# wq and w1 in one load each, 128 rows of w2 on four DMA engines, and softmax sums carried in the o product

## The chip, the cores and the metric

The kernel runs on one core of a Trainium2 chip. The metric is the device time of one execution in microseconds (us), the median of several runs. The engines are TensorE (PE), VectorE (DVE), ScalarE (ACT), GpSimd (POOL) and SyncE (SP). SP issues nearly all transfers here; 16 DMA engines carry them out.

## What is computed

The reference is one decode step of a layer whose attention and MLP stand side by side: x + A(xn) + B(xn), with xn the layernorm of x. x has 2 rows (B = 2) of D = 576.

```python
xn = (x - mean(x)) / sqrt(var(x) + 1e-5)
# A: attention over the last W = 2048 positions of the caches; 32 query heads share 16 kv heads
q = xn @ wq                                # [576, 4096]
p = softmax(q @ k.T * 128 ** -0.5)         # k, v: 2 x 16 heads x 2048 x 128
A = (p @ v) @ wo                           # [4096, 576]
# B: MLP with a squared relu
h = relu(xn @ w1 + b1) ** 2                # [576, 4608]
B = h @ w2 + b2                            # [4608, 576]
```

All inputs and the output are bf16.

## The kernel before, in words

**Units.** Attention is cut into 8 units (`NU`), each of 4 kv heads of one of the two rows; a unit's k and v are one DMA of 2 MB each into one of 6 buffers of `kvpool`. For unit u, `step(u)` (line 473) transposes k on PE as pairs of bf16 seen as f32 (32 matmuls into `kT_ps`, 3 PSUM buffers, line 289), copied out by ACT and DVE in turn (lines 297 and 299), multiplies it with the queries (`scores`), and forms the softmax (`softmax`, line 316): a maximum per partition on DVE (`mx`), a maximum over partitions on POOL (`gmax`), `nb` on DVE, exp on ACT (`pr`, with its row sums), and a 32x32 transpose on DVE (`pT`).

**The product with v** lags two units behind. `pv_sum(u)` (line 337) adds the softmax sums over partitions with an f32 matmul with `samec`, takes the reciprocal (`ri`) and makes the factors `f`. `pv(u, i)` multiplies into `pv_ps`, one PSUM buffer. `pv_mix(u)` (line 359) brings four parts together on DVE, each with its column of `f`: instructions `acc` at lines 365 and 368. `pv_out(u)` (line 377) puts the result in head order into `sm` by an f32 matmul with `tohead`; after every fourth unit `od` and `ws` are formed from it on DVE, and `wo_acc` (line 393) multiplies with one half of wo into `out_ps`. `sm` is one PSUM buffer, shared by units 0 to 3 and then by units 4 to 7.

**The weights wq and w1** (576 rows) are loaded by `issue_w` (line 114) in three DMAs: 512 rows at 4 rows to a partition in two DMAs of two rows each, and the last 64 rows as two half rows (`wq_rem`, `w1_rem`, named `w_rem` in the trace). `q_block(c)` (line 254) and `mlp_h_block(c)` (line 407) multiply each of the five pieces as it comes.

**The MLP.** `mlp_h_end` (line 415) takes relu on ACT and the square on DVE into `hrow` (bf16), transposes it in 9 PE instructions (`ha`), and copies it to `hT_sb`. w2 is in 4 groups of 9 rows to a partition. The first three go into `out_ps` (`mlp_o`), which is copied to `part` (line 541). The last group comes in two DMAs (7 and 2 rows to a partition) and goes into `tail_ps` (`mlp_tail`), where `part` is added by matmuls with the identity. Two engines copy `tail_ps` out and store it (lines 548 to 553).

**Order.** PE's instructions keep the order of the program text (`pe_mm` and `pe_tr`, lines 89 to 93, which is why most matmuls have the line 90 or 93), and so do the instructions of `pv_mix`. The other engines' order is made by the tile scheduler. SP issues in the order k0, wq, k1, v0, k2, v1, k3, then one v and one k for each step as buffers come free, wo's first half, w1, the last k, v and v, wo's second half, and w2. After `step(6)` stand `mlp_h_start`, the products of units 4 and 5, `wo_acc(0)`, h, `step(7)`, the products of units 6 and 7, `wo_acc(1)`, and w2 (lines 524 to 546).

Of the kernel before, what the change touches and what calls it, by code (L numbers as in the profile page):

```python
# [11 lines left out]
ALU = mybir.AluOpType  # L12
# [4 lines left out]
def kernel(  # L17
# [39 lines left out]
    NFULL = D // P  # L57
    RW = 2
    REM = D - NFULL * P
    S = P // REM  # L60
    KC = NFULL + 1
    NXN = NFULL + S
    LQ = (Hq * Dh) // S
    L1 = F // S
    NG4 = 4
    QW = Hq * Dh // NG4
    QB = QW // 2
    QH = QW // Dh
# [3 lines left out]
    RB = 32 * (NG4 - 1) + B  # L72
# [9 lines left out]
    wbig = ctx.enter_context(tc.tile_pool(name="wbig", bufs=NFULL // RW))  # L82
    wrem = ctx.enter_context(tc.tile_pool(name="wrem", bufs=1))
# [14 lines left out]
    k_tiles, v_tiles, wq_tiles, w1_tiles, wo_tiles, w2_tiles = {}, {}, {}, {}, {}, {}  # L98
    WBW = max(Hq * Dh, F)
    WRW = max(LQ, L1)  # L100
# [13 lines left out]
    def issue_w(tiles, wt, i, name, width, lrem):  # L114
        if i < NFULL // RW:
            tl = wbig.tile([P, RW * WBW], BF16, tag="wbig", name=f"{name}_{i}")
            rows = wt[0:NFULL * P, :].rearrange("(p r) n -> p (r n)", r=NFULL)
            nc.sync.dma_start(out=tl[:, 0:RW * width], in_=rows[:, i * RW * width:(i + 1) * RW * width])
            for r in range(RW):
                tiles[i * RW + r] = tl[:, r * width:(r + 1) * width]  # L120
        else:
            tl = wrem.tile([P, WRW], BF16, tag="wrem", name=f"{name}_rem")
            nc.sync.dma_start(out=tl[:, 0:lrem], in_=wt[NFULL * P:D, :].rearrange("r (s l) -> (r s) l", s=S))
            tiles[NFULL] = tl

    def issue_wq(c):
        issue_w(wq_tiles, A_wq, c, "wq", Hq * Dh, LQ)

    def issue_w1(c):
        issue_w(w1_tiles, B_w1, c, "w1", F, L1)  # L130

    def w_rows(tiles, c, col0, n, L):
        if c < NFULL:
            return tiles[c][:, col0:col0 + n], c
        sg = col0 // L
        assert (col0 + n - 1) // L == sg
        return tiles[c][:, col0 - sg * L:col0 - sg * L + n], NFULL + sg
# [9 lines left out]
    def issue_w2(g, r0, r1):  # L147
        if g < NG4 - 1:
            tl = kvpool.tile([P, FR * D], BF16, tag="kv", name=f"w2_{g}")[:]
        else:  # L150
            if r0 == 0:
                w2_last.append(wbig.tile([P, FR * D], BF16, tag="wbig", name=f"w2_{g}"))
            tl = w2_last[0][:, r0 * D:r1 * D]
        rows = B_w2[g * HW:(g + 1) * HW, :].rearrange("(p r) n -> p (r n)", r=FR)
        nc.sync.dma_start(out=tl, in_=rows[:, r0 * D:r1 * D])
        w2_tiles[(g, r0)] = tl

    x_sb = const.tile([B, D], BF16, name="x_sb")
    nc.scalar.dma_start(out=x_sb[:], in_=x2d)
# [6 lines left out]
    NW = NFULL // RW + 1  # L166
    for i in range(NW):
        issue_wq(i)
    ones_f = const.tile([P, P], F32, name="ones_f")
    nc.vector.memset(ones_f[:], 1.0)  # L170
    col_f = const.tile([P, P], F32, name="col_f")
# [12 lines left out]
    ones_b = const.tile([1, B], BF16, name="ones_b")  # L184
    nc.vector.memset(ones_b[:], 1.0)
# [3 lines left out]
    for i in range(2):  # L189
        nc.vector.bn_stats(out=stats[:, i, :], in_=x_sb[:, i * half_d:(i + 1) * half_d])  # L190
# [6 lines left out]
    xn_sb = const.tile([B, D], BF16, name="xn_sb")  # L197
    nc.vector.tensor_scalar(out=xn_sb[:], in0=x_sb[:], scalar1=mv[:, 0:1], scalar2=rstd[:, 0:1],  # L198
                            op0=ALU.subtract, op1=ALU.mult)
    xr_sb = const.tile([B, S, P], BF16, name="xr_sb")  # L200
    nc.vector.memset(xr_sb[:], 0.0)
    for sg in range(S):
        nc.vector.tensor_copy(out=xr_sb[:, sg, sg::S], in_=xn_sb[:, NFULL * P:D])

    pro_ps = psum.tile([P, NXN, B], BF16, tag="misc", name="pro_ps")
    for c in range(NFULL):
        pe_tr(out=pro_ps[:, c, :], in_=xn_sb[:, c:NFULL * P:NFULL], identity=ident[:B, :B])
    for sg in range(S):
        pe_tr(out=pro_ps[:, NFULL + sg, :], in_=xr_sb[:, sg, :], identity=ident[:B, :B])
    xnT = const.tile([P, NXN, B], BF16, name="xnT")  # L210
    nc.vector.tensor_copy(out=xnT[:], in_=pro_ps[:])
# [21 lines left out]
    samec = const.tile([P, P // NC, NC], F32, name="samec")  # L233
    nc.gpsimd.tensor_copy(out=samec[:], in_=own[:].unsqueeze(1).to_broadcast([P, P // NC, NC]))
    tohead = const.tile([P, NC, DW], F32, name="tohead")
    nc.gpsimd.tensor_copy(out=tohead[:], in_=own[:].unsqueeze(2).to_broadcast([P, NC, DW]))
    qz = const.tile([P, 2, NU, 2, 4, NC], BF16, name="qz")
# [16 lines left out]
    def q_block(c):  # L254
        for k in range(2):
            for g in range(NG4):
                rhs, xc = w_rows(wq_tiles, c, g * QW + k * QB, QB, LQ)
                pe_mm(q_ps[k][32 * g:32 * g + B, :], lhsT=xnT[:, xc, :], rhs=rhs,
                                 start=(c == 0), stop=(c == KC - 1), skip_group_check=True,
                                 tile_position=(0, 32 * g))  # L260
        if c == KC - 1:
            qrow = const.tile([RB, QW], BF16, tag="row", name="qrow")
            nc.vector.tensor_copy(out=qrow[:, 0:QB], in_=q_ps[0][0:RB, :])
            nc.scalar.copy(out=qrow[:, QB:QW], in_=q_ps[1][0:RB, :])
            qT_ps = psum.tile([P, QH, P], BF16, tag="misc", name="qT_ps")
            for i in range(QH):
                pe_tr(out=qT_ps[:, i, 0:RB], in_=qrow[:, i * Dh:(i + 1) * Dh],
                                    identity=ident[0:RB, 0:RB])
            qT_v = qT_ps[:].rearrange("p i (g s) -> p i g s", s=32)
            for b in range(B):  # L270
                nc.vector.tensor_copy(out=qT_all[:, b, :].rearrange("p (g i) -> p i g", g=NG4), in_=qT_v[:, :, :, b])
            qe_ps = psum.tile([P, 2 * NU, NC], F32, tag="sm", name="qe_ps")
            for e in range(2):
                pe_mm(qe_ps[:, e * NU:(e + 1) * NU, :], lhsT=par[:, e, :, :].rearrange("p a i -> p (a i)"),
                                 rhs=qT_all[:].rearrange("p b h -> p (b h)"), start=True, stop=True)
            for a, cp in ((0, nc.vector.tensor_copy), (1, nc.scalar.copy)):
                lo, hi = a * (P // 2), (a + 1) * (P // 2)
                for w in range(2):
                    cp(out=qz[lo:hi, :, :, w, 2 * w + a, :].rearrange("p e u c -> p (e u) c"), in_=qe_ps[lo:hi, :, :])

    kT_tiles, sc_tiles, pT_tiles, sum_tiles, sm_tiles = {}, {}, {}, {}, {}
# [34 lines left out]
    def softmax(u):  # L316
# [12 lines left out]
        sums = keep.tile([P, 1], F32, tag="sums", name=f"sums_{u}")  # L329
        nc.scalar.activation(out=pr[:], in_=sc_ps, func=ACT.Exp, bias=nb[:], scale=scale, accum_out=sums[:])  # L330
        pT = keep.tile([P, NT, 32], BF16, tag="pT", name=f"pT_{u}")
        nc.vector.transpose(out=pT[:].rearrange("p t m -> p (t m)"), in_=pr[:])  # L332
        pT_tiles[u], sum_tiles[u] = pT, sums
# [3 lines left out]
    def pv_sum(u):  # L337
        tq, b = divmod(u, B)
        if u % (2 * B) == 0:
            sm_tiles[tq // 2] = psum.tile([P, B * Dh + 2 * B], F32, tag="sm", name=f"sm_{tq // 2}")  # L340
        rs = sm_tiles[tq // 2][:, B * Dh + u % (2 * B):B * Dh + u % (2 * B) + 1]
        pe_mm(rs, lhsT=samec[:].rearrange("p x c -> p (x c)"), rhs=sum_tiles.pop(u)[:],
                         start=True, stop=True, skip_group_check=True)
        f = work.tile([P, 4], F32, tag="f", name=f"f_{u}")
        ri = work.tile([P, 1], F32, tag="ri", name=f"ri_{u}")
        nc.vector.reciprocal(out=ri[:], in_=rs)
        nc.vector.tensor_scalar(out=f[:], in0=own_j[:], scalar1=ri[:, 0:1], scalar2=None, op0=ALU.mult)
        pv_cur[u] = (psum.tile([P, 4, Dh], F32, tag="misc", name=f"pv_ps_{u}"), f)

    def pv(u, i):  # L350
        pv_ps, f = pv_cur[u]
        v = v_tiles[u][:].rearrange("p (w t x) -> p t w x", w=2, t=NT)
        for k in range(4):
            t = 4 * i + k
            pe_mm(pv_ps[32 * k:32 * (k + 1), :, :].rearrange("m (w a) d -> m w (a d)", w=2),
                                  lhsT=pT_tiles[u][:, t, :], rhs=v[:, t, :, :], start=(i == 0),
                                  stop=(i == NT // 4 - 1), skip_group_check=True, tile_position=(0, 32 * k))

    def pv_mix(u):
        pv_ps, f = pv_cur[u]  # L360
        acc = None
        for j in range(4):
            nx = work.tile([P, Dh], F32, tag=f"acc{j % 2}", name=f"acc_{u}_{j}")
# [220 lines left out]
```

## Time and profile before

| what | value |
|---|---|
| median of 9 runs (lowest, highest) | 134.63 us (134.44, 135.23) |
| the profiled execution: time, span | 134.62 us, 132.8 us |
| PE busy | 92.9 us, 70% of the span |
| DVE, ACT, POOL busy | 61.6, 46.4, 7.4 us |
| moved by the DMA engines | 53.74 MB, mean 405 GB/s |
| mean granted clock of PE | 0.871 |

The profile is of one execution on the chip; its span is from the first to the last instruction that it shows. Busy time is not the same as what sets the end: for that the chain of waits is followed back from the last instruction, and the rows in order of time tell when each instruction started, how long it took, and what ended the idle time before it. A matmul's row has a start and a duration; several in a row are merged, with their count behind "x". "PEld" is a load of the stationary operand, which overlaps PE. The granted clock is the share of full speed at which PE was allowed to run in a stretch.

### The profile page before, as it was taken

Reading aid. Unit: us, or ns where it says so; the run is one execution under the profiler, and the core shown is the slowest. Engines: PE = TensorE matmul, PEld = TensorE weight load, DVE = VectorE, ACT = ScalarE, POOL = GpSimd, SP = SyncE. Lnnn points to the kernel's source line nnn. Section 1 sums busy time; section 2 is a strip of 40 time slices with the busy share of each in tenths; the row PEclk is TensorE's granted clock in tenths of the full one; section 3 lists DMA queues with packets and bytes.
Section 4 is the critical chain, followed back from the end, with each engine's and each line's share of the span. In section 5 each row is a group of like instructions: output and inputs, shape, how many; then the busy total and the mean of one; then the engine's idle time right before and its main releaser. Section 6 shows DMA issues by size and latency. Waiting matters only on the chain.

```text
span 132.8 us, 2075 instructions
## 1 busy us (share of the span) xinstructions
PE 92.9 (70%) x846; PEld 56.4 (42%) x846; DVE 61.6 (46%) x169; ACT 46.4 (35%) x63; POOL 7.4 (6%) x20
## 2 busy tenths in 40 slices
PE   0059744986499779779689619977967973829761
PEld 0059412753464535445345305434526931305530
DVE  6914404455424665664763761367322448260021
ACT  6705503394353355364373253332032542000001
POOL 7500000100100010010000100001000001000000
PEclk9999999599658999999999975698698699555999
DMA  4999999999999999999999999999999999999940
GB/s 149 386 432 429 429 434 419 434 424 434 427 434 429 434 429 424 434 429 434 419 424 439 427 443 427 427 433 427 418 439 419 439 428 433 417 428 425 420 203 1
DMA packets 4260, 53.74 MB, mean 405 GB/s; under 512 B 530, under 2 KB 536, under 8 KB 1052
## 3 DMA queue, kind: packets, MB, share of 16 engines
q1 hardware_dynamic: 4180, 53.61, 95.0%
q8 instruction: 6, 0.10, 0.3%
q0 software_dynamic: 64, 0.01, 0.0%
q14 instruction: 2, 0.02, 0.0%
q10 hardware_dynamic: 8, 0.00, 0.0%
HBM read 53.62 MB, written 0.00 MB: 404 GB/s over the span
## 4 chain that ended last, share of the span: by engine, by line
DMA 46%; PE 32%; DVE 9%; issue 3%; ACT 3%; SPq 2%; POOL 1%; ACTq 0%; POOLq 0%
DMA w<-in_B_w_dram 23%; DMA k<-in_A_k_cache_dram 23%; PE kT_ps L93 15%; PE sc_ps L90 6%; PE pv_ps L90 5%; DVE kT L299 3%; DVE mx L319 3%; PE out_ps L90 2%; ACT kT L297 2%; PE h_ps L90 2%; SPq L111 1%; DVE acc L368 1%; PE sm L90 1%; POOL gmax L323 1%; PE tail_ps L90 1%
## 5 line engine op out<-in xcount | busy, mean ns | idle before, releaser
L93 PE MATMUL kT_ps<-ident_f,k 128*128 128x128 f32 x256 | 44.6, 326 | 5.5 <-DMA k<-in_A_k_cache_dram 3.8
L297 ACT COPY kT<-kT_ps 128x1024 bf16<-128x1024 bf16 x32 | 31.9, 1012 | 31.5 <-PE kT_ps L93 31.5
L93 PEld LDWEIGHTS kT_ps<-ident_f,k 128*128 128x128 f32 x256 | 34.9, 167 | 18.1 <-issue 8.1
L299 DVE COPY kT<-kT_ps 128x1024 bf16<-128x1024 bf16 x32 | 22.0, 687 | 31.2 <-PE kT_ps L93 31.2
L90 PE MATMUL sc_ps<-kT,qz 128*32 128x512 bf16 x128 | 9.8, 388 | 6.4 <-DVE kT L299 5.5
L90 PE MATMUL pv_ps<-v,pT 128*32 128x512 bf16 x128 | 13.7, 472 | 0.0
L330 ACT ACTIVATE pr<-sc_ps,nb 128x512 bf16<-128x512 f32 x8 | 5.5, 687 | 20.4 <-DVE nb L327 20.3
L90 PE MATMUL sm<-acc,tohead 128*64 128x128 f32 x16 | 3.9, 333 | 6.9 <-DVE acc L368 6.9
L323 POOL PARTITION_ALL_REDUCE gmax<-m x8 | 2.9, 366 | 101.8 <-DVE m L321 82.0
L368 DVE SCALAR_TENSOR_TENSOR acc<-pv_ps,f,acc 128x128 f32<-128x128 f32 x24 | 8.3, 346 | 0.5
L332 DVE STREAM_TRANSPOSE pT<-pr 128x512 bf16<-128x512 bf16 x8 | 5.7, 709 | 4.8 <-ACT pr L330 4.8
L90 PE MATMUL out_ps<-wo,ws 128*2 128x288 bf16 x64 | 7.1, 407 | 1.1 <-DVE ws L390 1.1
L319 DVE TENSOR_REDUCE mx<-sc_ps 128x1 f32<-128x512 f32 x8 | 5.5, 692 | 3.5 <-PE sc_ps L90 3.1
L552 ACT CAST fin_sb<-tail_ps 2x144 bf16<-2x144 f32 x2 | 0.5, 273 | 17.8 <-PE tail_ps L90 17.8
L90 PEld LDWEIGHTS <-qz 128*32 128x32 bf16 x128 | 2.1, 94 | 10.1 <-DVE kT L299 7.1
L90 PEld LDWEIGHTS <-ws 128*2 128x2 bf16 x64 | 3.8, 118 | 4.7 <-DVE ws L390 1.5
L90 PEld LDWEIGHTS sm<-acc,tohead 128*64 128x64 f32 x16 | 1.7, 152 | 9.6 <-DVE acc L368 8.8
L90 PE MATMUL sm<-sums,samec 128*128 128x1 f32 x16 | 3.5, 289 | 2.8 <-DVE od L386 2.8
L90 PEld LDWEIGHTS <-pT 128*32 128x32 bf16 x128 | 3.2, 99 | 4.4 <-issue 3.9
L93 PE MATMUL pro_ps<-ident,xn_sb 2*128 2x2 bf16 x4 | 0.3, 172 | 6.7 <-DVE xn_sb L198 6.7
L90 PEld LDWEIGHTS sm<-sums,samec 128*128 128x128 f32 x16 | 3.0, 238 | 4.5 <-DVE od L386 3.0
L541 DVE COPY part<-out_ps 2x288 f32<-2x288 f32 x2 | 0.9, 448 | 7.9 <-PE out_ps L90 7.9
(86 smaller groups left out, 63.2 us busy)
## 6 DMA issues: line engine op xcount, KB each, us to landing
k<-in_A_k_cache_dram SPq DMA_DIRECT2D x8, 2048.0 KB, 22.2
v<-in_A_v_cache_dram SPq DMA_DIRECT2D x8, 2048.0 KB, 26.0
wo<-in_A_wo_dram SPq DMA_DIRECT2D x2, 2304.0 KB, 22.6
w<-in_B_w_dram SPq DMA_DIRECT2D x2, 2304.0 KB, 29.9
wq<-in_A_wq_dram SPq DMA_DIRECT2D x2, 2048.0 KB, 14.0
w<-in_B_w_dram SPq DMA_DIRECT2D x3, 1296.0 KB, 26.3
w<-in_B_w_dram SPq DMA_DIRECT2D x1, 1008.0 KB, 30.9
w_rem<-in_B_w_dram SPq DMA_DIRECT2D x1, 576.0 KB, 33.3
```

What stands on the lines that cost most here:

```text
L90: return tc.keep_in_program_order(nc.tensor.matmul(out, **kw))
L93: return tc.keep_in_program_order(nc.tensor.transpose(**kw))
L111: return [lambda i=i: nc.sync.dma_start(out=tl[:, i * n:(i + 1) * n], in_=v[:, :, i * n:(i + 1) * n]) for i in range(parts)]
L297: nc.scalar.copy(out=dst, in_=src)
L299: nc.vector.tensor_copy(out=dst, in_=src)
L319: nc.vector.tensor_reduce(out=mx[:], in_=sc_ps, axis=AX.X, op=ALU.max)
L323: nc.gpsimd.partition_all_reduce(gmax[:], m2[:], channels=P, reduce_op=ReduceOp.max)
L330: nc.scalar.activation(out=pr[:], in_=sc_ps, func=ACT.Exp, bias=nb[:], scale=scale, accum_out=sums[:])
L332: nc.vector.transpose(out=pT[:].rearrange("p t m -> p (t m)"), in_=pr[:])
L368: op = nc.vector.scalar_tensor_tensor(out=nx[:], in0=pv_ps[:, j, :], scalar=f[:, j:j + 1], in1=acc[:], op0=ALU.mult, op1=ALU.add)
L541: nc.vector.tensor_copy(out=part[:, i * OH:(i + 1) * OH], in_=out_ps[32 * i:32 * i + B, :])
L552: cp(out=fin_sb[:, q * OQ:(q + 1) * OQ], in_=mlp["out"][32 * k:32 * k + B, :])
```

## The change

wq and w1 become one DMA each. A weight matrix of 576 rows is seen as 1152 half rows, 9 to each of the 128 partitions, in one contiguous run; an odd and an even half row can belong to the same row of the matrix, so `xnT` holds 9 columns for each of two halves, with zeros where a partition's half row belongs to the other. The products of the two halves come out in different rows of PSUM (4 rows where there were 2). For q they are added within a matmul in f32 with a selection matrix (`sel_q`); for h, `hrow` is f32 and is transposed in f32, and `add_halves` adds the halves behind it; relu and square follow in one DVE instruction.

The last 128 rows of w2 leave the last group (now 8 rows to a partition, in DMAs of 6 and 2). They go into `w2x_sb`, 48 partitions of which 32 are used, by two DMAs that ACT issues early, with an outermost dimension of 4 on the side of the source. Their part of h is copied apart (`hx`), and eight matmuls (`mlp_x`) add their product to `out_ps` ahead of the other groups.

The softmax sums are stored as a 129th column beside the mixed product (`acc`), and the matmul with `tohead` carries them; the reciprocal is taken once in four units, and `od` is formed by two instructions. `pv_sum`, `samec`, `f` are gone; `pv_mix` takes the factors `own_j`. Biases and x are added in one product with `res_b`, and b1 and b2 are loaded through ACT's queue.

```diff
-    def issue_w(tiles, wt, i, name, width, lrem):
...
+    def issue_w(wt, name, width):
+        tl = wbig.tile([P, HP * FL], BF16, tag="wbig", name=f"{name}_sb")
+        nc.sync.dma_start(out=tl[:, 0:HP * width], in_=wt.rearrange("d (s l) -> (d s) l", s=2)
+                          .rearrange("(p r) l -> p (r l)", r=HP))
+        w_tiles[name] = tl
...
+    def q_all():
+        w = w_tiles["wq"]
+        for k in range(HP):
             for g in range(NG4):
+                o = k * QL + g * QB
+                pe_mm(q_ps[k % 2][32 * g:32 * g + 2 * B, :], lhsT=xnT[:, k, :, :].rearrange("p a b -> p (a b)"),
+                      rhs=w[:, o:o + QB], start=(k < 2), stop=(k >= HP - 2), skip_group_check=True,
+                      tile_position=(0, 32 * g))
+        qrow = const.tile([RB, 2, QB], F32, tag="row", name="qrow")
...
+        for i in range(QH):
+            for k in range(2):
+                pe_mm(qs_ps[:, i, :], lhsT=qrow[:, k, i * Dh:(i + 1) * Dh],
+                      rhs=sel_q[0:RB, k, :, :, :].rearrange("p b h g -> p (b h g)"), start=(k == 0), stop=(k == 1))
...
-    def pv_sum(u):
...
+    def pv_start(u):
+        pv_cur[u] = psum.tile([P, 4, Dh], F32, tag="misc", name=f"pv_ps_{u}")
...
+        if u % (2 * B) == 0:
+            sm_tiles[t] = psum.tile([P, B, Dh + 1], F32, tag="sm", name=f"sm_{t}")
         sm = sm_tiles[t]
+        pe_mm(sm[half * (P // 2):(half + 1) * (P // 2), b, :],
+                         lhsT=tohead[:].rearrange("p c x -> p (c x)"), rhs=acc_tiles.pop(u)[:], start=True, stop=True,
...
+    def mlp_h_all():
+        w = w_tiles["w1"]
+        for k0 in range(0, HP, 2):
+            for t in range(3):
+                for k in range(k0, min(k0 + 2, HP)):
+                    for g in range(2):
...
+        for k in range(3):
+            nc.scalar.copy(out=hrow[:, k * HB:(k + 1) * HB], in_=mlp["ps"][k][0:RB, :])
...
+        for r0, n in ((0, 5), (5, FR - 5)):
+            ps = psum.tile([P, 5, RB], F32, tag="sc", bufs=2, name=f"ha_ps_{r0}")
+            for r in range(n):
+                pe_tr(out=ps[:, r, :], in_=hrow[:, r0 + r:HW:FR], identity=ident_f[0:RB, 0:RB])
+            add_halves(ps, P, n, ((0, 2, three(0, r0, n)),
+                                  (2, 1, hs[:, 2 * FR + r0:2 * FR + r0 + n, :].unsqueeze(2))))
+        for r0, n in ((0, 5), (5, FT - 5)):
+            ps = psum.tile([P, 5, RB], F32, tag="kT", bufs=3, name=f"hb_ps_{r0}")
...
+    def mlp_x():
+        for r in range(XR):
+            out_acc(mlp["h"][0:XP, N3 + FT + r, :], lambda a, z: w2x_sb[:, r * D + a:r * D + z])
...
-    W2P = [(0, 0, 9), (1, 0, 9), (2, 0, 9), (3, 0, 7), (3, 7, 9)]
+    W2P = [(0, 0, 9), (1, 0, 9), (2, 0, 9), (3, 0, 6), (3, 6, 8)]
...
+    for h in range(2):
+        n = XE * 2 * XI * XR
+        nc.scalar.dma_start(out=w2x_sb[32 * h:32 * h + XE * XI, :],
+                            in_=B_w2[FX0:FX0 + n, :].rearrange("(e h i r) n -> h e i (r n)", h=2, i=XI, r=XR)[h])
```

## The prediction

> **What bounds the kernel now.** I read the page first, then the chain that ended last, then the order of time of the last 45 us, and last a table of narrow windows over the end of the DMA stream. On the page the transfers look like the bound: one queue keeps 16 DMA engines busy for 95.0% of the span.
>
> ```profile
> q1 hardware_dynamic: 4180, 53.61, 95.0%
> ```
>
> That is 53.61 MB / 16 = 3.35 MB per DMA engine in 126.2 us, 26.6 GB/s each. The chain of waits agrees at its end: its last long piece is the DMA of w2, then 3.4 us of work that no transfer covers.
>
> ```profile
> 97.84 30.85 DMA w<-in_B_w_dram
> 128.69 0.04 issue
> 128.74 1.29 PE tail_ps L90 x44
> ```
>
> But a bound that ends last can be closely followed. These rows, from the order of time of the end, have start, duration, engine, line, and in brackets the idle time before and its releaser:
>
> ```profile
> 97.68 0.69 PE L90 MATMUL h_ps<-w_rem,xnT 128*2 128x384 bf16 x8
> ...
> 100.42 0.74 PE L93 MATMUL ha_ps<-ident,hrow 98*128 98x98 bf16 x9 [2.05 <-DVE hrow L421]
> ...
> 101.68 4.48 PE L93 MATMUL kT_ps<-ident_f,k 128*128 128x128 f32 x24 [0.16 <-DMA k<-in_A_k_cache_dram]
> ...
> 119.78 3.51 PE L90 MATMUL out_ps<-wo,ws 128*2 128x288 bf16 x32 [1.13 <-DVE ws L390]
> ...
> 126.31 1.27 PE L90 MATMUL out_ps<-w,hT_sb 128*2 128x288 bf16 x18 [0.82 <-DMA w<-in_B_w_dram]
> 127.61 0.93 DVE L541 COPY part<-out_ps 2x288 f32<-2x288 f32 x2 [7.89 <-PE out_ps L90]
> 128.74 0.61 PE L90 MATMUL tail_ps<-w,hT_sb 128*2 128x144 bf16 x28 [1.16 <-DMA w<-in_B_w_dram]
> ```
>
> From the end of h (98.37) PE waits for a DMA only 0.16 us (the last k), then 0.82 us (third w2 group), then at the tail. Without the last two waits: the third group runs 125.49 to 126.76, part is copied by 127.7, the last 16 matmuls (0.42 and 0.30 us) end near 128.5. They end at 129.93. So **the compute chain from h to the end is only 1.4 us shorter than the DMA stream**: that is the whole cover for work added behind h.
>
> **The change, part by part.** The times are of the profiled execution (134.62 us; span 132.8, so 1.8 us lie around it), 0.01 us under the median of 134.63.
>
> *DMA.* The bytes stay. Of w2's last group, 128 rows of 1152 B (147 KB) leave the 16 engines for four: 9.2 KB less on each, 0.35 us at 26.6 GB/s, and 36.9 KB more on four, 1.39 us; these four net +1.04 us. wq and w1 become 9 pieces a partition in one run, so four DMAs and 512 packets go. The trace has no packet of 36 KB; bounds for its rate are nothing and 0.2 us gained for all engines (w1's 18,432 B took 687 ns each, its remainder's 4,608 B 178 ns, so about 8 ns of a packet are not bytes; 32 packets per engine, 0.2 us). I take 0.2. Whether this shortens the stream depends on which engines are the four:
>
> ```profile
> 127.00:127.25 0.25, 0.25 (x8) 0.18 (x6) 0.00 (x0) 0.00 (x0) 0.00 (x0) 1.00 0.98 401
> 127.25:127.50 0.25, 0.25 (x6) 0.01 (x2) 0.00 (x0) 0.00 (x0) 0.00 (x0) 1.00 0.54 217
> 128.50:128.75 0.25, 0.01 (x4) 0.01 (x5) 0.04 (x1) 0.00 (x0) 0.00 (x0) 1.00 0.28 111
> ```
>
> The last two columns are the DMA share and GB/s: half of the engines are done by 127.4, others 1.5 us later. If the four are early ones, the stream ends up to 0.55 us sooner (0.35 + 0.2); if a late one is among them, 1.04 - 0.2 = 0.8 us later. The trace doesn't name them. The Trainium skill ("DMA: Bandwidth & Descriptors", Rules for kernel authors) speaks against this edit: an outermost dimension under 16 confines a DMA to that many engines. Taken alone it gives the +0.8; no run here shows which engines.
>
> *q at the start.* Before, 32 of 40 matmuls of q were done before the last part of wq came; now 36 matmuls follow the landing, 36 x 64 ns = 2.3 us (16 took 1.03) against 0.60 for the last 8; 8 f32 products of pairs (0.38 us a pair in the row of sums) cost 3.0 us for 0.52. With the 1.39 us that the extra rows can delay wq, q is 4 to 6 us later. I cost it at nothing at the end: PE waited 2.1 us for k at 35 us, then ran at a low clock, and two more covers follow at 77 and 96 us (next). A k or v is issued some 22 us before it lands, so its later issue doesn't empty the queue. Without the cover it costs 4 to 6.
>
> *Sums.* Eight f32 matmuls with reciprocal and product go. In the steps they stand beside the softmax, not in the chain. But one of them waits for od, because sm is one buffer (the order of time, PE alone):
>
> ```profile
> 76.17 0.43 PE L90 MATMUL sm<-acc,tohead 128*64 128x128 f32 x2 [0.43 <-DVE acc L368]
> 79.37 0.59 PE L90 MATMUL sm<-sums,samec 128*128 128x1 f32 x2 [2.77 <-DVE od L386]
> ...
> 80.44 1.12 PE L93 MATMUL kT_ps<-ident_f,k 128*128 128x128 f32 x4
> ...
> 85.19 0.66 PE L93 MATMUL kT_ps<-ident_f,k 128*128 128x128 f32 x4
> ```
>
> After 2.77 us of idling the same four transposes took 1.12 us, and 0.66 only from 85 us on. The stall goes, and with it this slow stretch: 2.8 + about 3 us. PE then finishes with wo's first half near 89 us instead of 95.5, and **meets the next late thing: w1**, whose last part landed 33.3 us after its issue at 63.4, at 96.7. So it is no gain; it makes a 5 to 7 us pause.
>
> *h.* All 54 matmuls now follow the whole w1, at 96.5 (96.7 - 0.2). Warm they take 54 x 42 ns (45 took 1.91) = 2.3 us; after a pause the trace's factor is 1.12/0.66 = 1.7, 3.9 us. I take 3.9, since the pause is longer than the 2.77 us that slowed PE above; with 0.3 us for the last one h ends near 100.8, **+2.4** (bounds +0.8 and +3.8, the latter if w1 is held by the four engines' 1.39). The skill ("TensorE: Matmul & The Clock Gate", Part 1) has the clock halved after an idle window of about 3.4 us; here 2.8 us sufficed. By its factor of 2 the h term would be 0.7 us more.
>
> *Behind h.* hrow becomes three ACT copies, 1.4 us (two took 0.87, one 0.49) for 2.05: **-0.6**. Nine bf16 transposes (0.74) become 21 f32 ones of hrow and hx; by the row of kT (8 in 1.04 in the chain) 2.7 us: **+2.0**. PE has nothing else, and pv_out and the whole last step are queued behind them, so k is no longer late: **-0.2**. The halves' additions run on ACT and DVE beside the transposes; they hold the PSUM buffers of the last step by under 0.5 us, at most that more.
>
> *Last softmax.* Both sums matmuls (0.38, 0.59) go, but DVE's order changes: pT now stands ahead of all four parts of pv_mix(6), where three ran before it. pT ended at 113.03, so the mix ends at 114.5 (1.5 us, as 116.40 to 117.90), not 113.26; after pv_out, pv(7) starts at 115.15 instead of 114.45, +0.7; od in two instructions with a reciprocal, 0.85 for 0.42, +0.4. Together **+1.0** (bounds -0.5, if the mix still runs first, and +1.3).
>
> *w2's extra rows.* Eight more out_ps matmuls at 70 ns (18 in 1.27) to 110 ns (32 in 3.51), **+0.6**; four fewer in the tail lie beside part.
>
> Sum: 2.4 - 0.6 + 2.0 - 0.2 + 1.0 + 0.6 = 5.2 us behind h, less the cover of 1.4: **+3.8, 138.4 us**. The DMA stream, within 0.8 us of its old end, isn't last any more.
>
> **The rivals.** (1) *PE stays warm in h*, because q's delay lasts and it arrives late, or short waits don't slow it: 1.6 us less, 136.8. For it: in 26 of 40 slices the clock is 0.9 or more; against it: the pause above. (2) *The DMA stream stays the bound*, and the four engines are early ones: it ends 0.3 to 0.55 sooner, 134.2, faster. It decides only if the work behind h grows by less than the 1.4 us of cover, so if transposes, h and mix are all priced too high. The half of the engines that is idle at 127.4 speaks for it, the 21 transposes against it. (3) *The change does nothing at the end*: the same cover, but the four engines' gain is taken by a late one, 134.6. (4) *The four engines hold w1 back* by 1.39 on top of the forecast: 139.8.
>
> **How the numbers follow.** Forecast 0.43, rival 1 0.25, rival 2 0.13, rival 3 0.07, rival 4 0.12. A measurement of this kernel tells 0.2% (0.27 us) from no change, so faster is rival 2 (0.13), within 0.2% rival 3 (0.07), slower the rest, 0.80. The range reaches from 134.3, which leaves most of rival 2 out, to 139.8, which cuts rival 4 in half.
>
> **What would show it.** Right: PE idle for over 4 us before the first h matmul, at a clock near 0.5 then; the first transposes of the last k at 105 us, not 101.7; no DMA wait before the third w2 group; part copied after the last w2 landing. The sums' wait for od at 77 us is gone. Wrong: tail matmuls still released by the w2 DMA, h done by 99.5, or pv_mix(6) ahead of pT on DVE.

## The result and the profile after

The changed kernel takes 137.59 us (median of 10 runs, 135.6 to 138.8) against 134.63 for the kernel before (30 runs, 134.39 to 135.32), so by the medians it is 2.96 us slower. The ratio is 1.0183, 95% interval 1.0157 to 1.0209; here and below a ratio leaves out the runs that lie over 1.5% above the fastest of their kernel (here three of the ten, from 137.63 up), so this one stands for 2.5 us. The profiled execution that came with the result took 138.82 us, 1.2 above the median; the readings below are from a later one of the same kernel at 137.45 us (span 135.7), the nearer of the two to the median.

The page's row of the main queue (packets, MB, share of 16 engines) answers to the 95.0% of before:

```profile
q1 hardware_dynamic: 3604, 53.46, 92.5%
```

576 packets fewer, 147 KB less on this queue, and 16 engines that aren't busy to the end any more. The chain that ended last, in order of time (start, duration), says the same:

```profile
65.29 31.83 DMA w_sb<-in_B_w_dram
97.16 4.34 PE h_ps L89 x50
...
123.65 7.18 PE out_ps L89 x89
132.15 0.74 PE tail_ps L89 x12
```

Before, a DMA of w2 reached from 97.84 to 128.69 in this chain. Now no transfer stands behind 97.16: h, its transposes, the last unit, wo, w2 and the tail follow one another. PE's rows in order of time (start, duration, then the idle time before and its releaser in brackets):

```profile
97.16 4.96 PE L89 MATMUL h_ps<-w_sb,xnT 128*4 128x384 bf16 x54 [3.47 <-DMA w_sb<-in_B_w_dram]
102.81 1.28 PE L92 MATMUL ha_ps<-ident_f,hrow 100*128 100x100 f32 x9 [0.69 <-ACT hrow L406]
103.93 1.05 PE L92 MATMUL hb_ps<-ident_f,hrow 100*128 100x100 f32 x8
104.82 0.51 PE L92 MATMUL hx_ps<-ident_f,hx 100*48 100x100 f32 x4
...
105.62 1.53 PE L92 MATMUL kT_ps<-ident_f,k 128*128 128x128 f32 x12
...
123.65 3.50 PE L89 MATMUL out_ps<-wo,ws 128*2 128x288 bf16 x32 [1.52 <-DVE ws L374]
127.08 0.65 PE L89 MATMUL out_ps<-w2x_sb,hT_sb 48*2 48x288 bf16 x8
127.66 3.23 PE L89 MATMUL out_ps<-w,hT_sb 128*2 128x288 bf16 x50
...
131.67 0.89 PE L89 MATMUL tail_ps<-part,ident_f 2*2 2x144 f32 x8 [0.16 <-DVE part L567]
132.49 0.30 PE L89 MATMUL tail_ps<-w,hT_sb 128*2 128x144 bf16 x8
```

h starts at 97.16, the last k's first transposes at 105.62 (101.68 before), wo's second half at 123.65 (119.78), the end is at 132.79 (129.93). None of PE's rows behind h waits for a DMA. The end of the stream, in narrow windows (last two columns: DMA share, GB/s):

```profile
128.50:128.75 0.25, 0.25 (x8) 0.17 (x4) 0.00 (x0) 0.00 (x0) 0.00 (x0) 1.00 0.14 55
128.75:129.00 0.25, 0.25 (x8) 0.17 (x4) 0.00 (x0) 0.00 (x0) 0.00 (x0) 1.00 0.03 9
```

By its packets it ends at 128.91, before at 128.97. So the transfers are as late as they were, and the work of PE, DVE and ACT behind w1 has become longer than they are.

### The profile page after: what moved, and what is told of

It reads as the page before. It is cut to its first block, busy times and chain, and to the rows that moved or that the text cites. A ratio compares the mean times of both kernels' runs of the same rounds, so it can differ in the third digit from the quotient of the medians.

```text
span 137.0 us, 2079 instructions
## 1 busy us (share of the span) xinstructions
PE 94.0 (69%) x846; PEld 54.1 (39%) x846; DVE 60.6 (44%) x157; ACT 46.8 (34%) x68; POOL 9.7 (7%) x28
## 4 chain that ended last, share of the span: by engine, by line
DMA 37%; PE 37%; DVE 10%; ACT 8%; issue 4%; SPq 1%; POOL 1%; POOLq 0%; ACTq 0%; DVEq 0%
DMA w_sb<-in_B_w_dram 24%; DMA wq_sb<-in_A_wq_dram 14%; PE kT_ps L92 11%; PE out_ps L89 6%; PE sc_ps L89 5%; ACT kT L281 5%; PE h_ps L89 3%; PE pv_ps L89 3%; PE q_ps L89 3%; ACT pr L314 2%; DVE kT L283 2%; DVE mx L303 2%; DVE mix L345 1%; PE qs_ps L89 1%; PE sm L89 1%
## 5 line engine op out<-in xcount | busy, mean ns | idle before, releaser
L92 PE MATMUL kT_ps<-ident_f,k 128*128 128x128 f32 x256 | 40.4, 303 | 4.7 <-ACT kT L281 4.7
L92 PEld LDWEIGHTS kT_ps<-ident_f,k 128*128 128x128 f32 x256 | 30.9, 154 | 16.7 <-issue 8.7
L89 PE MATMUL sc_ps<-kT,qz 128*32 128x512 bf16 x128 | 10.5, 414 | 6.5 <-DVE kT L283 4.7
L89 PE MATMUL pv_ps<-v,pT 128*32 128x512 bf16 x128 | 12.8, 447 | 0.0
L89 PE MATMUL sm<-acc,tohead 128*64 128x129 f32 x16 | 4.1, 341 | 8.2 <-DVE acc L345 8.2
L89 PEld LDWEIGHTS <-xnT 128*4 128x4 bf16 x90 | 3.1, 119 | 13.7 <-issue 13.7
L89 PE MATMUL h_ps<-w_sb,xnT 128*4 128x384 bf16 x54 | 5.0, 521 | 3.9 <-DMA w_sb<-in_B_w_dram 3.9
L89 PE MATMUL q_ps<-wq_sb,xnT 128*4 128x512 bf16 x36 | 3.8, 605 | 5.1 <-DMA wq_sb<-in_A_wq_dram 5.1
L92 PE MATMUL pro_ps<-ident,xs 2*128 2x2 bf16 x10 | 0.6, 164 | 8.1 <-DVE xs L181 8.1
L345 DVE SCALAR_TENSOR_TENSOR mix<-pv_ps,own_j,mix 128x128 f32<-128x128 f32 x16 | 5.6, 348 | 0.4
```

Source lines behind the costliest of these rows:

```text
L89: return tc.keep_in_program_order(nc.tensor.matmul(out, **kw))
L92: return tc.keep_in_program_order(nc.tensor.transpose(**kw))
L345: op = nc.vector.scalar_tensor_tensor(out=nx, in0=pv_ps[:, j, :], scalar=own_j[:, j:j + 1], in1=acc, op0=ALU.mult, op1=ALU.add)
```

## The experiments

Theory: the chain of compute from w1's landing to the end has become the bound; it grew in h, in the transposes, in the last softmax and in w2's products. Rivals: the four engines hold the transfers back; the sums are the cost; the low clock in h has another cause than PE's pause.

### The sums alone

In the kernel before:

```diff
+        acc = keep.tile([P, Dh + 1], F32, tag="acc", bufs=4, name=f"acc_{u}")
...
-        pe_mm(rs, lhsT=samec[:].rearrange("p x c -> p (x c)"), rhs=sum_tiles.pop(u)[:],
```

> Kernel before with the softmax sums alone changed (129th column, od in two instructions); loads, h and w2 as before. Theory (the chain of compute behind h has become the bound, the sums give only 1.0 us of it): the last step grows by 1.0 us, which the 1.4 us of cover under the w2 transfers hides, the wait for od at 77 us goes but is no gain: 134.6 (within 0.3). Rival 1 (the sums' removal is worth something by itself, 2.8 + 3 us of PE come out): 133 or less. Rival 2 (the sums cost most of the loss): 136.5 or more.

134.68 us, ratio 0.9999 (0.998 to 1.0018). In its profile w2's third group and the tail are the last rows of note:

```profile
124.07 4.33 PE L90 MATMUL out_ps<-w,hT_sb 128*2 128x288 bf16 x54
128.68 0.61 PE L90 MATMUL tail_ps<-w,hT_sb 128*2 128x144 bf16 x28 [0.29 <-DMA w<-in_B_w_dram]
```

The tail is still released by the w2 DMA, but it waits 0.29 us for it instead of 1.16. So the sums alone cost nothing in the time, as expected, and the stall at 77 us that goes with them is worth nothing at the end. That the last step grows by 1 us isn't shown by this profile. DVE has the changed kernel's order in it, and PE waits 4.14 us for `acc` instead of 2.58; but the last products with v took 1.40 us and not 1.90, and from the last scores to wo's second half it is 10.64 us where it was 10.34. The rest of what the cover lost came with the products of wo and w2 (4.00 and 4.33 us, before 3.51 and 3.64).

### Without the rows on four engines

```diff
-    W2P = [(0, 0, 9), (1, 0, 9), (2, 0, 9), (3, 0, 6), (3, 6, 8)]
+    W2P = [(0, 0, 9), (1, 0, 9), (2, 0, 9), (3, 0, 7), (3, 7, 9)]
...
-    mlp_x()
```

w2x_sb, its loads and hx go with it, and 9 transposes of hrow serve all four groups.

> Changed kernel without the w2 rows on four engines: w2's last group has 9 rows again, 9 f32 transposes of hrow instead of 21, no hx, no mlp_x. Theory: the chain behind h loses 12 transposes (1.05 + 0.51 us in the changed kernel's rows) and 8 products (1.12 us), 2.7 us in all, so from 137.6 down to the end of the transfers: 134.9 (134.5 to 135.5), with the tail released by the w2 DMA again. Rival 1 (the late, whole w1 and its slow products are the loss, the extra transposes lie beside other work): 136.8 or more. Rival 2 (the four engines are what makes the stream or wq late): also near 134.6, but then h starts earlier than 97.2 us, by up to 1.4 us.

135.62 us, ratio 1.0076 (1.0049 to 1.0103): 2 us of the 3 come back. The tail waited 0.58 us for the w2 DMA, as the theory has it. Not all that came back is the rows' work: from the start of ha to the last k's transposes it is 1.57 us instead of 2.81, and the eight products (0.65 us) are gone, but h too took 2.60 us in this profile and not 4.96. And the time is 0.7 above what the theory gave. A reason for that is in the packets: those of 10,368 B took 399 ns in the mean instead of 389, and the stream ended at 129.77. By the sizes of the tiles, each rounded up to 32 bytes, the buffers of k, v and the weights had moved: taken modulo 256, they start 32 bytes ahead of their place in the kernels before and after. So:

```diff
+    pad = const.tile([P, 8], F32, name="pad")
```

> The changed kernel without the w2 rows on four engines once more, with an unused tile of 32 bytes ahead, so that the buffers of k, v and the weights start at multiples of 64 bytes as in the kernels before and after; in the first run they started 32 bytes off, and the packets of 10,368 B took 393 to 402 ns instead of 389. Theory (the placement slowed the transfers by 0.8 us, the compute chain itself fits under them): 389 ns again, the last w2 landing near 129.4, 134.7 (134.4 to 135.0). Rival (135.6 is compute behind h): 135.4 to 135.8 again.

136.06 us (4 runs, 134.52 to 136.51), ratio 1.012 (1.0091 to 1.015). The packets took 389 ns again, as the theory said, and the stream ended at 128.59, 0.38 us sooner than in the kernel before. The profiled execution took 134.52, with the tail released by the DMA:

```profile
96.39 4.28 PE L88 MATMUL h_ps<-w_sb,xnT 128*4 128x384 bf16 x54 [2.13 <-DMA w_sb<-in_B_w_dram]
...
128.35 0.61 PE L88 MATMUL tail_ps<-w,hT_sb 128*2 128x144 bf16 x28 [0.24 <-DMA w<-in_B_w_dram]
```

But the median missed the 134.7, and the rival's 135.8 too; it is no better than without the pad (135.62), and what the placement gave shows in the lowest run alone (134.52, without the pad 135.36). The other three of the four runs took 1.3 to 2 us more than the profiled one. The chain of compute is only 0.24 us shorter than the stream here, so whatever lengthens it shows, and its rows aren't of one length: h took 4.28 us here and 2.60 in the profile with the shifted buffers, the 54 products of w2 3.47 here and 4.52 there. What sets them is told below; which of them was long in the three runs without a profile isn't known.

### Keeping PE busy in the pause ahead of h

```diff
+    for i in range(44):
+        pe_mm(mlp["ps"][i % 3][0:4, 0:256], lhsT=zz[:], rhs=par[:].rearrange("p e a i -> p (e a i)"),
+              start=False, stop=False, skip_group_check=True, tile_position=(0, 0))
     mlp_h_all()
```

> Changed kernel with 44 extra matmuls of zeros into h_ps (256 columns each, about 2.7 us warm and 4.3 us at the low clock) between wo's first half and h, so that PE doesn't idle while it waits for w1; they add zeros to the result. Theory (the pause of 3.85 us before h lowers the clock; h takes 4.96 us for 54 products, 92 ns each, against 42 ns in the kernel before): h takes 2.3 to 3 us and the end comes 1.6 to 2.6 us sooner, 135.0 to 136.0. Rival (the products are slow for their own reasons, by their shape or order): h still takes about 5 us, 137.5 or up to 0.5 more.

137.81 us (4 runs), ratio 1.0177 (1.0101 to 1.0253): no gain, because the 44 products were mis-sized. They took 0.113 us each (h's 0.048), 4.75 us for 42 of them in a row, and held h back to 99.4; h itself then ran in 2.60 us. With 16 of them:

> Changed kernel with 16 extra matmuls of zeros into h_ps (256 columns, 0.113 us each in the run with 44, so 1.8 us) in the pause before h, and buffers at multiples of 64 bytes; they add zeros to the result. Theory (a pause of 3.85 us before h halves the clock, one of about 2 to 3.3 us doesn't: h took 4.96 us after 3.85, 2.60 us after 2.35 and after 3.26): h takes 2.6 us in each run and the end is 1.2 to 2.4 us sooner than 137.6: 135.2 to 136.4. Rival (the clock in h goes by something else, and the median of the changed kernel has a fast h already): 137.6.

136.83 us (4 runs), ratio 1.0181 (1.0134 to 1.0229): above the theory's range.

```profile
94.82 1.91 PE L89 MATMUL h_ps<-par,zz 128*4 128x256 bf16 x16
98.12 2.60 PE L89 MATMUL h_ps<-w_sb,xnT 128*4 128x384 bf16 x54 [1.39 <-DMA w_sb<-in_B_w_dram]
```

h took 2.60 us, so its 4.96 is the clock and not the shape of its products; that rival is out. Nearly half of the gain of 2.4 us is eaten by w1, whose first product starts at 98.12 instead of 97.16: this kernel's buffers start 64 bytes past their place in the changed kernel, and the stream ended at 129.88. More went at the end: from wo's second half to the last tail product it is 10.40 us (121.76 to 132.16), in the changed kernel 9.14. The extra products with the buffers in their old place and DVE's order left as it was were not run.

### The order on DVE in the last softmax

```diff
-    step(NU - 1, with_pv=False)
+    last_pT = step(NU - 1, with_pv=False)
     pv_all(NU - 2)
+    last_pT()
```

step(7) does all of the softmax but its transpose, which last_pT() writes behind pv_mix(6).

> Changed kernel with one instruction moved on DVE: the transpose to pT of the last unit stands behind three parts of pv_mix(6), as before the change, not ahead of all four. Theory (the order of DVE in the last softmax costs 0.7 us on the path that sets the end): 136.9, 0.4 to 0.8 sooner than the changed kernel. Rival (pv(7) waits for something else, or the transfers end last): no change, 137.6.

134.74 us (10 runs, 134.52 to 136.83), ratio 1.0011 (0.9981 to 1.004): nearly all of the loss is gone (2.85 us by the medians), where 0.7 was expected. DVE's rows, first of the kernel before (where the mix writes to `acc` throughout), then of the changed kernel, then of this one:

```profile
111.30 0.34 DVE L365 TENSOR_SCALAR acc<-pv_ps,f 128x128 f32<-128x128 f32 x1
111.67 0.74 DVE L368 SCALAR_TENSOR_TENSOR acc<-pv_ps,f,acc 128x128 f32<-128x128 f32 x2
112.33 0.70 DVE L332 STREAM_TRANSPOSE pT<-pr 128x512 bf16<-128x512 bf16 x1
112.95 0.31 DVE L368 SCALAR_TENSOR_TENSOR acc<-pv_ps,f,acc 128x128 f32<-128x128 f32 x1
```

```profile
115.08 0.71 DVE L316 STREAM_TRANSPOSE pT<-pr 128x512 bf16<-128x512 bf16 x1 [0.91 <-ACT pr L314]
115.72 0.31 DVE L342 TENSOR_SCALAR mix<-pv_ps,own_j 128x128 f32<-128x128 f32 x1
116.06 0.74 DVE L345 SCALAR_TENSOR_TENSOR mix<-pv_ps,own_j,mix 128x128 f32<-128x128 f32 x2
116.83 0.35 DVE L345 SCALAR_TENSOR_TENSOR acc<-pv_ps,own_j,mix 128x128 f32<-128x128 f32 x1
```

```profile
112.11 0.34 DVE L342 TENSOR_SCALAR mix<-pv_ps,own_j 128x128 f32<-128x128 f32 x1
112.49 0.74 DVE L345 SCALAR_TENSOR_TENSOR mix<-pv_ps,own_j,mix 128x128 f32<-128x128 f32 x2
113.14 0.70 DVE L317 STREAM_TRANSPOSE pT<-pr 128x512 bf16<-128x512 bf16 x1
113.77 0.31 DVE L345 SCALAR_TENSOR_TENSOR acc<-pv_ps,own_j,mix 128x128 f32<-128x128 f32 x1
```

From the start of the last k's transposes to wo's second half it is 16.91 us (103.64 to 120.55) instead of 18.03: the order is worth 1.1 us. The other 2.0 us in these two profiles lie before: h took 2.60 us here, not 4.96, and the transposes of k began at 103.64, not 105.62. So two terms of 1.1 and 2.0 together pass the 2.9 us by which the chain was too long, and in this profile the transfers are last again:

```profile
97.22 2.62 PE h_ps L89 x54
99.86 28.73 DMA w<-in_B_w_dram
128.63 1.46 PE tail_ps L89 x40
```

The edit doesn't touch anything ahead of h. That h was quick in this execution is the clock's matter (below), and it began early. From 24.1 to 27.5 us the granted clock was 0.50 here and 1.00 in the changed kernel's profile, and the 16 products that add the halves of q took 3.57 us instead of 1.93. So PE was later all the way: wo's first half ended at 94.87 and not at 93.69, and the pause ahead of h was 2.35 us and not 3.47. Why most of this kernel's runs are near 134.7 and most of the changed kernel's near 137.5, when the 1.1 us alone would set them 1.1 apart, isn't settled: the place of the clock's slow stretches is known for the profiled runs only.

### w1 in two loads

```diff
-            issue_w(B_w1, "w1", FL)
+            issue_w(B_w1, "w1", FL, ((0, 6), (6, 9)))
```

> Changed kernel with w1 loaded in two DMAs, six and three of the nine half rows, so that 36 of the 54 products of h can run before the last part lands. Theory (h waits for the whole of w1 and then runs at a low clock): the 36 run in the pause, the last 18 take 0.9 to 1.7 us behind the landing, h ends 1.7 to 3 us sooner than 102.1: 134.9 to 136.0. Rival (h's place costs nothing, the chain starts with the transposes or later): 137.2 or more.

136.35 us (10 runs, 134.44 to 137.15), ratio 1.007 (1.0019 to 1.0121): outside both ranges, nearer the theory's 136.0.

```profile
97.19 1.14 PE L89 MATMUL h_ps<-w_sb,xnT 128*4 128x384 bf16 x18 [1.87 <-DMA w_sb<-in_B_w_dram]
99.34 1.72 PE L92 MATMUL ha_ps<-ident_f,hrow 100*128 100x100 f32 x9 [1.01 <-ACT hrow L407]
100.85 1.54 PE L92 MATMUL hb_ps<-ident_f,hrow 100*128 100x100 f32 x8
```

h ends 3.8 us sooner, at 98.33. The half clock came later, from 99.55 to 102.96 (in the changed kernel's profile from 95.77 to 102.60): the 21 transposes take 4.1 us instead of 2.8, and the last k's begin 2.3 us sooner, at 103.35. So h's start and its clock are on the path, and the low clock moved with PE's idle time.

### The rows on four engines, alone

In the kernel before, with 19 bf16 transposes behind h where 9 were (ten more, not the eleven of the expectation):

```diff
+    XE, XI, XR = 4, 8, 2
...
+    W2P = [(0, 0, 9), (1, 0, 9), (2, 0, 9), (3, 0, 6), (3, 6, 8)]
```

> Kernel before with the 128 w2 rows on four DMA engines alone, as 64 partitions of 2 rows (64 packets of 2,304 B, 9.2 KB less on each of 16 engines, 36.9 KB more on four) and 11 more bf16 transposes behind h, 4 products ahead of w2; sums and the loads of wq and w1 as before. Theory (the stream doesn't end sooner, since the four engines take the place of the late ones; in the changed kernel it ended at 129.24 against 129.40): 134.6, within 0.3. Rival 1 (the edit shortens the stream and only the compute chain hides it): 134.2 or less. Rival 2 (four late engines): 135.2 or more.

136.46 us (4 runs), ratio 1.0152 (1.0117 to 1.0187). The tail is released by the w2 DMA, 1.0 us later than before (128.74), and the stream ends at 130.10, 1.13 later:

```profile
129.74 0.55 PE L95 MATMUL tail_ps<-w,hT_sb 128*2 128x144 bf16 x24 [0.34 <-DMA w<-in_B_w_dram]
```

The second rival's number came, but its reason didn't. The whole stream was late, on all engines: wq's last packet ended at 21.00 instead of 19.05, and 16 packets were in flight until 127.8 us, before until 127.1. From 10 to 20 us, while the small packets ran, 193 packets took over 5 ns more than their usual time, 0.71 us on each engine; in the changed kernel, with half as many packets of 4,608 B, 10 did. And the four engines weren't the late ones. At 128.3 us six packets were in flight in the kernel before, so six engines were late; in the changed kernel ten were at 127.8, and here ten at 128.6. The DMA share (second column from the right) tells much the same, before and here:

```profile
128.00:128.40 0.40, 0.00 (x0) 0.00 (x0) 0.37 (x2) 0.00 (x0) 0.00 (x0) 1.00 0.31 121
```

```profile
127.20:127.70 0.50, 0.50 (x12) 0.36 (x10) 0.00 (x0) 0.00 (x0) 0.00 (x0) 1.00 1.01 415
128.30:129.00 0.70, 0.70 (x16) 0.48 (x14) 0.00 (x0) 0.00 (x0) 0.00 (x0) 1.00 0.58 230
```

So the four belonged to the ten that were done early, and the extra bytes made late ones of them too. The remaining 0.4 us of the loss lie outside the span (2.2 us around it instead of 1.8), for which I have no cause.

### The changed kernel again, and what mends it

> The changed kernel itself, unchanged, beside the next three. Theory (the clock of PE is set anew every 3.413 us from how busy PE was in the window before, on a grid whose place against the kernel differs from run to run; h falls into a slow window or not): single runs in steps between 135.6 and 138.8, most of them 136.4 to 137.6. Rival (the steps belong to the chip or the hour of the first runs): one level, within 0.3.

137.86 us (6 runs, 137.38 to 138.81), ratio 1.0233 (1.0191 to 1.0276). Three runs lie at 137.4 to 137.7 and three at 138.1 to 138.8: more than the one level of the rival, but higher than forecast, and the quick runs of 135.6 and 136.6 didn't come again. A spread of 1.4 us doesn't set this kernel apart: the next three spread by 1.5 to 1.6, with most of their runs within about 0.5.

> Changed kernel with pT of the last unit behind three parts of pv_mix(6) on DVE and 20 extra matmuls of zeros (2.3 us) in the pause before h; buffers at multiples of 128 bytes; the extra matmuls add zeros to the result. Theory (a slow h and the order on DVE, 2.4 and 1.1 us, are what the compute chain is too long by; without both the transfers end last again): 134.6, nearly every run between 134.4 and 135.1, none at 136.8. Rival (the extra rows or transposes are too long by themselves): 135.5 or more.

134.81 us (12 runs, 134.43 to 135.92), ratio 1.0002 (0.9977 to 1.0028). With the order on DVE and 20 products in the pause, all parts of the change stand in the kernel, and it takes the time of before; no run is near 136.8, where two of the ten with the order alone were. The theory's two terms suffice for that. That the transfers end last again isn't shown: in its profile (134.89 us) no row of PE behind w1 waits for a DMA, the products into out_ps end at 128.56 and the stream at 128.82.

> Changed kernel without the w2 rows on four engines (9 transposes instead of 21, no products ahead of w2), with pT of the last unit behind three parts of pv_mix(6), buffers at multiples of 128 bytes. Theory (whole loads of wq and w1 end the stream 0.38 us sooner, 128.59 against 128.97, the rows on four engines gave that back; the chain now fits under the transfers even with a slow h): 134.2 to 134.5, hardly a run above 135. Rival (the stream's end varies by as much anyway): 134.6 to 134.8.

134.47 us (12 runs), ratio 0.9982 (0.9957 to 1.0007).

> The same with 20 extra matmuls of zeros (2.3 us) in the pause before h, which add zeros to the result. Theory (h at full clock in each run): as the run without them in its fast runs, 134.2 to 134.4, with the slow ones gone. Rival (the extra matmuls delay h or cost as much as they save): 134.6 or more.

134.43 us (12 runs), ratio 0.999 (0.9964 to 1.0016). In both the stream ends sooner, at 128.67 and 128.62 (128.97 before), and the first of them carries even a slow h:

```profile
96.58 4.30 PE h_ps L88 x54
100.89 27.50 DMA w<-in_B_w_dram
128.43 1.29 PE tail_ps L88 x44
```

The medians lie 0.16 and 0.20 us under 134.63, but both intervals hold 1: a gain over the kernel before isn't shown.

## Why the prediction was right

Direction, place and mechanism held: the range (134.3 to 139.8) held 137.59, and most of what was to be seen was seen. PE paused 3.47 us ahead of h (forecast over 4, since wo's first half was to end near 89 us and ended at 93.69) and ran at half clock behind it; the last k's first transposes came at 105.6 (105); no DMA wait stood before the third w2 group; part was copied at 131.17, after the last landing; the stall at 77 us was gone. q was 5.9 us later (first scores at 28.79, before 22.89; forecast 4 to 6) and cost nothing at the end, since PE still waited for w1.

The sizes, from the kernel before (134.62) to the execution at 137.45:

| step | forecast | measured | from |
|---|---|---|---|
| end of h | +2.4 | +3.75 | 98.37 to 102.12 |
| hrow copies | -0.6 | -1.36 | 2.05 to 0.69 us |
| transposes, and k's wait | +1.8 | +1.55 | ha's start to the last k: 1.26 to 2.81 us |
| last k's transposes and scores | 0 | -1.14 | 7.76 to 6.62 us |
| last softmax to wo | +1.0 | +1.07 | 10.34 to 11.41 us |
| wo to the end | +0.6 | +0.42 | 8.72 (without DMA waits) to 9.14 us |
| cover | -1.4 | -1.43 | 129.93 less 128.5 |
| sum | +3.8 | +2.86 | 137.45 less 134.62 is 2.83 |

Three terms were mis-sized, not all in one direction. **h** was late by 1.35 us more. w1 was to land 0.2 us sooner by its larger packets; its last packet ended at 96.78, 0.4 later than before (96.36), and without the rows on four engines at 96.20: they cost w1 0.6 us, a part of what rival 4 gave them. And the 54 products took 4.96 us, 1.9 times their 2.60, not 3.9; the factor of 1.7 had been read from transposes. **The hrow copies** gave 0.76 us more, as they began at 101.52, before h's last products ended. **The last unit's step** was left out: the prediction showed the 24 transposes of 4.48 us, but didn't ask at which clock. Before, they ran at half clock for 3.4 us; in the changed kernel they ran at full clock. These windows (PEclk is the third column from the right) are of the kernel before, then of the changed one:

```profile
102.20:105.60 3.40, 3.40 (x18) 3.40 (x17) 1.38 (x2) 2.02 (x2) 0.00 (x0) 0.50 1.00 429
```

```profile
106.00:109.40 3.40, 3.17 (x28) 2.40 (x30) 1.80 (x3) 2.82 (x3) 0.00 (x0) 1.00 1.03 442
```

So a slow stretch came in h, and one that was on the path before went. That the sum came so near is in part luck: the mechanism was right, but the terms missed by +1.35, -0.76, -1.14 and smaller amounts, which cancel to -0.94.

The larger packets do give what was estimated: 36,864 B took 1364 ns where two of 16,384 and one of 4,096 took 1381, 17 ns for each of 8 packets of an engine, and as much for w1: 0.27 us in all (forecast 0.2). The stream without the rows on four engines ended 0.30 to 0.38 us sooner. The rows, which were to gain 0.35 on 12 engines, cost 0.24 to 0.32 of that again at the stream's end. The four engines were early ones, for which the prediction had the stream up to 0.55 us sooner; it ended 0.06 sooner. What the prediction left out is that an engine done less than 1.0 us ahead of the last, with 1.0 us more to do, becomes the last itself. And from 128.69 to the end of the span it is 4.1 us, not the 3.4 that the prediction reads there; the sum doesn't use them.

## What to carry to other kernels

Where the compute behind the last transfers is nearly as long as they are, an edit is priced by that cover: here the sums cost nothing alone, and the order on DVE that came with them 1.1 us beside the slower h. One transpose that moved ahead of three short instructions on DVE was worth 1.1 us of path, more than anything that this change saves on the transfers (0.3 us), so compare the order of the last stage's instructions on every engine. And ask of each stretch at which clock it ran, before and after: work that makes PE wait can be paid again behind the wait.

## What the hardware showed

**The clock of PE goes by a fixed grid.** In 14 profiles the granted clock was 1 or 0.5 and changed only on a grid of 3.413 us, whose place against the kernel differed from execution to execution. PE's busy share in one interval told the next (counted from the first clock on record, at 11 to 14 us): at full clock with PE busy under 0.42, all 33 next intervals were at half clock; between 0.42 and 0.55, 17 of 26; between 0.55 and 0.67, 6 of 44; above that 1 of 241. Back to full clock it never went from an interval under 0.82 busy (59), in 7 of 20 up to 0.92, and in 50 of 55 above. The changed kernel, and the one with the order mended, around the pause before h:

```profile
92.40:95.80 3.40, 1.29 (x22) 0.77 (x17) 0.17 (x1) 0.00 (x0) 0.00 (x0) 1.00 0.89 384
95.80:99.20 3.40, 2.04 (x28) 0.94 (x31) 0.00 (x0) 0.00 (x0) 0.00 (x0) 0.50 0.98 419
99.20:102.60 3.40, 2.92 (x34) 0.96 (x22) 0.00 (x0) 1.08 (x3) 0.00 (x0) 0.50 1.01 429
```

```profile
93.30:96.70 3.40, 1.57 (x26) 0.95 (x21) 0.65 (x2) 0.00 (x0) 0.00 (x0) 1.00 0.82 351
96.70:100.10 3.40, 2.60 (x54) 1.33 (x53) 0.00 (x0) 0.56 (x2) 0.00 (x0) 1.00 0.96 410
```

PE was busy 1.29 of 3.4 us (0.38) in the one and 1.57 (0.46) in the other, and h ran at half and at full clock. So a pause of 3.26 us did no harm where the grid cut it in two, and one of 2.13 us halved the clock where it fell into one interval. So where compute ends last, the time can differ from run to run by what such a stretch costs: the same 54 products of h took 2.60, 4.28 and 4.96 us in these profiles. That the steps between single runs come from it is likely, but isn't shown, since the intervals of the other runs aren't on record. The Trainium skill ("TensorE: Matmul & The Clock Gate", Part 1) has this free-running window of 3413 ns, and the grid agrees; it slows after an idle window, while here an interval that was 38% busy sufficed.

**Where a buffer starts in SBUF.** By the sizes of the tiles ahead of them, the k, v and weight buffers of ten kernels start at the same place modulo 256 bytes, and there at most 1% of the 16,384-B packets after 22 us took more than 612 ns. Starting 32 bytes ahead of that place, and 32 and 64 bytes past it, 84%, 79% and 61% did, and the streams ended 0.8 to 1.2 us later (129.77 against 128.59 for the same kernel without and with 32 bytes more ahead). The Trainium skill ("DMA: Bandwidth & Descriptors", How a descriptor splits into AXI transactions) tells that a descriptor which doesn't start at a multiple of 256 B begins with a piece from the multiple below it, and can so be cut into more pieces; the runs fit it if the common place is such a multiple, and no run here shows the pieces or the addresses.
